# Folding the second layer's DFT over columns a second time, with even and odd outputs side by side in the bank

## The chip, the cores and the metric

The kernel runs on one core of one Trainium2 chip. Its time is device microseconds of one execution; the profile is one further execution, recorded by the hardware profiler.

## The reference, cut to what matters

```python
def _A_ref(x, dft_seq_re, dft_seq_im, dft_hid_re, dft_hid_im):     # FNet mixing: Real(DFT_seq(DFT_hidden(x)))
    a = jnp.einsum("bsd,ed->bse", x, dft_hid_re)
    b = jnp.einsum("bsd,ed->bse", x, dft_hid_im)
    return jnp.einsum("ts,bse->bte", dft_seq_re, a) - jnp.einsum("ts,bse->bte", dft_seq_im, b)

def _B_ref(x, w_gate, w_up, w_down):                                # gated GLU
    g, u = x @ w_gate, x @ w_up
    return (sigmoid(g) * u) @ w_down

x = A_x                                    # 1 x 2048 x 640, float32; the GLU is 1728 wide
for _ in range(2):                         # two layers, the same matrices in both
    x = x + _A_ref(layernorm(x), ...)
    x = x + _B_ref(layernorm(x), ...)
```

## The kernel before, in words

The kernel takes the DFT matrices as inputs but uses their symmetries: cos(n) = cos(N - n), sin(n) = -sin(N - n). Whether the inputs really have them is tested on the chip beside the other work (the *tests*: a part of a matrix is loaded, mirrored parts are subtracted or added on DVE, and ACT sums the squares). A flag at the end decides whether a general, slow path must run; with these inputs it doesn't.

**Rows of x.** The 16 tiles of 128 rows are kept in four blocks of four tiles GA, GB, GC, GD, so that mirrored rows (t, S - t, S/2 - t, S/2 + t) lie on the same partition. Block 1 (`SP`) holds the rows that are their own mirror image, apart from the others in `row`.

**A layer's mixing, folded.** `fold_columns` adds and subtracts the mirrored columns of a row (321 sums `e`, 320 differences `o`, the EC and EH of the code), `fold_rows` normalizes and folds mirrored rows, `fold_join` folds them once more (GB and GD then hold what the even and the odd output rows need) and splits the result into two float16 parts, HI and LO. A float32 product is done as three float16 ones (`PASSES`: HI x HI, HI x LO, LO x HI). Then TensorE works in two steps. `sequence(i, tp)` (line 796) is the DFT over rows for block i, even (EV) or odd (OD) outputs: 18 matmuls of some 256 columns into three banks. Blocks 0 and 1 (ph 0) share banks, as do blocks 2 and 3 (ph 1). `evict_sums` takes the banks out into `z`, again as two parts (line 239 on DVE, line 237 on ACT). `hidden(q, ph)` (line 922 in `product`) is the DFT over columns: z as stationary operand, the 321 columns of the cosine or sine matrix (`h`) as moving operand, 18 matmuls into a pair of banks. `evict_hidden`, `join_hidden` (996) and `add_hidden` (1009) bring the result to x. `hidden_middle` is the same for the rows that are their own image.

Layer 1's mixing is the opening, in float32 for the first step, in an order written out by hand. It splits the cosine and sine matrices and stores the parts in DRAM (`drop_hidden`); layer 2 loads them back (`load_wh_again`).

**Order of the rest.** From then on `steps` is the list of TensorE's work with a planned duration for each step, and every other operation is set into that list, at a planned time (`when`, `run_at`) or at a step (`run`). Each engine runs its own instructions in this order. Layer 1 after its opening: gate and up products (steps "c"), the seven-product form of them ("j", line 1174, whose sums ACT copies out at line 1178 and DVE adds), then down-projections ("d", lines 1316, 1411, 1430; DVE adds to x in line 1304). During the second half of "j" blocks 0 and 1 are folded for layer 2 and stored (`spill`), during the last down-projection blocks 2 and 3. `he` is the index of the first step of layer 2's mixing, `b0` that of its first gate product:

```python
order = [(sequence, 0, EV), (sequence, 1, EV), (sequence, 0, OD), (sequence, 1, OD), (sequence, 2, EV),
         (sequence, 2, OD), (hidden, 0, 0), (sequence, 3, EV), (hidden, 1, 0), (sequence, 3, OD),
         (hidden, 0, 1), (hidden, 2, 0), (hidden, 3, 0), (hidden, 1, 1), (hidden, 2, 1), (hidden, 3, 1),
         (hidden_middle,)]
...
run_at(end + 3, [(fold_join, 3, ALL, (n,)) for n in range(3)])
...
run(he + 2, evictions(0, (EV,)))
```

All DMAs but a few go through one queue (SP). All buffers lie in one large tile in SBUF; `PLACES` lists, in the order of the requests, where each goes. There are eight banks of PSUM, handed out in the order in which they came free. The tests go over stretches of time (`spans`: from, to, weight), spread evenly over the weighted length; each loads in one slot, subtracts two slots later and squares 0.85 of a slot after that.

Of the kernel before, what the change touches and what calls it, by code (L numbers as in the profile page):

```python
# [17 lines left out]
P = 128  # L18
# [13 lines left out]
EC = EH + 1  # L32
EPS = 1e-5
# [8 lines left out]
XF = 2.0**8  # L42
CS = 2.0**14
ZS = 2.0**-1
# [62 lines left out]
273 327 208 343 402 172 367 336 237 332"""  # L107
# [95 lines left out]
def folded(ctx, tc, pool, dram, big, acc, flag, x, ct, wh, wg, wu, wc, wd, out):  # L203
# [5 lines left out]
    hs = pool.tile([P, 1], F32, name="hs")  # L209
    edge = pool.tile([P, 2], F32, name="edge")  # L210
# [100 lines left out]
    def start_identity():  # L311
        nc.vector.tensor_scalar(ident16, ramp, part[:, 34:35], None, op0=OP.is_equal)

        nc.vector.tensor_tensor(hs, ident16[:, 63:64], ident16[:, 64:65], op=OP.add)
        nc.vector.tensor_scalar(hs, hs, -0.5 * CS, CS, op0=OP.mult, op1=OP.add)
        drop("ramp")
        drop("part")
# [258 lines left out]

    def fold_stats(i, g):
        row_stats(quad_tile(i), g, 4 * i + g)
# [8 lines left out]
    def fold_columns(i, k):  # L587

        g = slice(2 * k, 2 * k + 2)
        e, o = (v[:, g] for v in folds(i))  # L590
        xg = X[:, 4 * i : 4 * i + 4, :][:, g]
        a, b = xg[:, :, 1 : EH + 1], xg[:, :, D - 1 : EH - 1 : -1]
        nc.vector.tensor_tensor(e[:, :, :EH], a, b, op=OP.add)
        nc.vector.tensor_tensor(o, a, b, op=OP.subtract)  # L594

    def fold_double(i, k):
# [3 lines left out]
        on.tensor_scalar(e[:, :, EH:], xg[:, :, 0:1], 2.0, None, op0=OP.mult)  # L600
# [43 lines left out]
    def fold_row(n):  # L644
# [5 lines left out]
        if n == 1:  # L650
            nc.vector.scalar_tensor_tensor(f[0:1, :EC], f[0:1, 384 : 384 + EC], t[0:1, GD, 19:20], f[0:1, :EC],
                                           op0=OP.mult, op1=OP.add)
        if n == 2:
            w = take(2, "fw").f16[:, :EC]
            nc.gpsimd.memset(w, 0.0)
            for p in (0, 64):
                nc.scalar.activation(w[p : p + 1], f[0:1, :EC], AF.Copy)
        if n == 3:
            w = held["fw"].f16[:, :EC]
            nc.vector.tensor_tensor(w[32:33], f[0:1, :EC], w[0:1], op=OP.subtract)  # L660
            drop("row")

# [4 lines left out]
    def fold_join(i, v=ALL, do=(0, 1, 2)):  # L667

        for n, (f, ops, fold, key, w) in enumerate(zip(folds(i), ((OP.add, OP.subtract), (OP.subtract, OP.add)),
                                                       (FE, FO), "eo", (EC, EH))):  # L670
            if n not in v:
                continue
            if 0 in do:
                for g, op in zip((GB, GD), ops):
                    nc.vector.tensor_tensor(f[:, g], f[:, GA], f[:, GC], op=op)
            if 1 in do:
                nc.scalar.activation(take_parts(key, i)[:, :, 0, :w], f[:, GB::2], AF.Copy)
                if n:
                    nc.gpsimd.memset(take_parts(key, i)[:, :, :, EH : EH + 1], 0.0)
            if 2 in do:  # L680
                p = take_parts(key, i)
# [1472 lines left out]
```

## Time and profile before

| what | value |
|---|---|
| time, median of 3 runs | 1104.82 us (1104.02 to 1105.79) |
| the profiled execution | 1106.03 us |
| its span in the trace | 1104.2 us |
| instructions | 17528 |
| TensorE busy | 1084.0 us, 6289 matmuls |
| DVE busy | 830.2 us |
| ACT busy | 572.9 us |
| granted TensorE clock | 0.998 |
| layer 2's mixing on TensorE | from 571.66 to 612.46 us of the span |

The span begins with the first recorded instruction. PE is the matmul part of TensorE, PEld its weight loads, which run beside the matmuls. In a line of a timeline stand start, length, engine, line of code, operation, output <- input, shape and count; an idle time before it, and what ended it, stands in brackets. Matmuls are pipelined, so that the length of a group is some 0.16 us longer than the time until the next group starts; in the chain of work the lengths are those up to the next piece. In a list of waits stand the total, the number and the longest.

### The profile page before, as it was taken

The numbers are of one execution on the slowest core, as the hardware profiler recorded it, in microseconds if no ns is written. First come the engines' busy times: TensorE is split into PE (matmuls) and PEld (weight loads), VectorE is DVE, ScalarE is ACT, GpSimd is POOL, SyncE is SP. The second block draws the span as 40 slices with busy tenths as digits, with TensorE's granted clock in tenths as the row PEclk, the third lists the DMA queues.
The fourth block names the chain that finished last, engine by engine and source line by source line (L and its number), as shares of the span: only waits on it lengthen the run. The fifth ranks groups of instructions, "written<-read, shape, count | busy, mean of one in ns | idle before, by whom it ended". The sixth has DMA issues, their size and how long they took to land.

```text
span 1104.2 us, 17528 instructions
## 1 busy us (share of the span) xinstructions
PE 1084.0 (98%) x6289; PEld 626.3 (57%) x6289; DVE 830.2 (75%) x1608; ACT 572.9 (52%) x1109; POOL 154.6 (14%) x250
## 2 busy tenths in 40 slices
PE   6999999999999999999999999999999999999997
PEld 3776444457774444457777844444677444444775
DVE  8996789868448999769887569895895356777962
ACT  7776547765315665555225544476761345555520
POOL 3110153312333151000110100012000010000010
PEclk9999999999999999999999999999999999999999
DMA  8414765366996877756742058645569856666521
GB/s 273 155 61 71 199 184 203 115 193 191 251 249 233 251 250 202 235 174 214 229 141 73 1 62 194 200 154 182 185 163 177 265 180 208 202 196 194 190 88 64
DMA packets 183079, 194.70 MB, mean 176 GB/s; under 512 B 76451, under 2 KB 145474, under 8 KB 182982
## 3 DMA queue, kind: packets, MB, share of 16 engines
q1 hardware_dynamic: 182342, 190.87, 58.8%
q0 software_dynamic: 640, 2.62, 0.6%
q8 instruction: 51, 0.84, 0.3%
q14 instruction: 46, 0.38, 0.1%
HBM read 145.29 MB, written 31.91 MB: 160 GB/s over the span
## 4 chain that ended last, share of the span: by engine, by line
PE 87%; DVE 8%; issue 2%; DMA 1%; ACT 1%; POOL 0%; SPq 0%; DVEq 0%; POOLq 0%; ACTq 0%
PE acc L1174 36%; PE acc L1430 17%; PE acc L1130 14%; PE acc L1316 8%; PE acc L922 4%; PE acc L1411 2%; PE acc L1283 2%; PE acc L834 2%; DVE big L642 1%; DMA big<-big 1%; DVE quad L424 1%; DVE big L239 1%; PE acc L796 1%; DVE big L1509 1%; DVE big L594 0%
## 5 line engine op out<-in xcount | busy, mean ns | idle before, releaser
L1174 PE MATMUL acc<-big 128*128 128x512 f16 x2160 | 467.8, 379 | 2.8 <-ACT big L1178 1.9
L1174 PEld LDWEIGHTS <-big 128*128 128x128 f16 x2160 | 211.3, 98 | 257.8 <-issue 3.5
L1430 PE MATMUL acc<-big 128*128 128x320 f16 x1512 | 213.2, 299 | 0.4 <-DVE big L1304 0.4
L1178 ACT ACTIVATE big<-acc 128x512 f32<-128x512 f32 x160 | 94.0, 593 | 191.9 <-PE acc L1174 167.5
L1430 PEld LDWEIGHTS <-big 128*128 128x128 f16 x1512 | 147.9, 98 | 58.5 <-issue 0.6
L1130 PE MATMUL acc<-big 128*128 128x512 f16 (+1 forms) x900 | 156.6, 336 | 0.0
L1130 PEld LDWEIGHTS <-big 128*128 128x128 f16 x900 | 87.9, 98 | 67.7 <-DVE big L239 0.2
L1481 ACT ACTIVATE big<-big 128x768 f32<-128x768 f32 (+6 forms) x106 | 79.0, 745 | 53.2 <-DVE big L1511 17.0
L1304 DVE SCALAR_TENSOR_TENSOR big<-acc,big 128x320 f32<-128x320 f32 x112 | 53.1, 485 | 53.7 <-PE acc L1411 27.2
L239 DVE SCALAR_TENSOR_TENSOR big<-big 128x640 f16<-128x640 f32 (+7 forms) x94 | 75.9, 830 | 22.5 <-ACT big L237 19.4
L1316 PE MATMUL acc<-big 128*128 128x320 f16 x656 | 89.3, 299 | 0.0
L1391 DVE TENSOR_TENSOR big<-big 128x512 f16<-128x512 f32 x126 | 85.3, 688 | 2.3 <-ACT big L1390 2.3
L1390 ACT ACTIVATE big<-big 128x512 f16<-128x512 f32 x126 | 74.0, 618 | 25.0 <-DVE big L1391 11.1
L237 ACT ACTIVATE big<-big 128x640 f16<-128x640 f32 (+9 forms) x94 | 63.8, 707 | 35.7 <-POOL big L1082 15.8
L1316 PEld LDWEIGHTS <-big 128*128 128x128 f16 x656 | 64.2, 98 | 25.1
L1224 DVE TENSOR_TENSOR big<-big,acc 128x512 f32<-128x512 f32 x40 | 27.3, 682 | 44.4 <-PE acc L1174 30.6
L516 ACT ACTIVATE big<-big 128x384 f16<-128x384 f32 (+2 forms) x56 | 36.0, 667 | 36.6 <-DVE big L501 17.2
L1181 ACT ACTIVATE big<-big 128x512 f32<-128x512 f32 x80 | 49.7, 622 | 9.7 <-DVE big L1224 6.6
L386 POOL DMA_INDIRECT out<-big,rows x8 | 8.6, 1070 | 310.9 <-DVE big L1304 173.5
L1509 DVE TENSOR_TENSOR big<-big 128x512 f32<-128x512 f32 x64 | 46.2, 722 | 5.9 <-DMA big<-in_ct 5.7
L1402 DVE TENSOR_TENSOR big<-big 128x512 f32<-128x512 f32 x72 | 50.1, 697 | 0.1
L439 POOL TENSOR_SCALAR rowt<-rowt 128x1 f32<-128x1 f32 x24 | 13.0, 540 | 242.4 <-ACT big L437 242.4
(199 smaller groups left out, 1230.2 us busy)
## 6 DMA issues: line engine op xcount, KB each, us to landing
big<-in_ct SPq DMA_DIRECT2D x256, 128.0 KB
big<-kept_f SPq DMA_DIRECT2D x63, 320.0 KB
big<-kept_S SPq DMA_DIRECT2D x33, 512.0 KB
big<-kept_w SPq DMA_DIRECT2D x33, 320.0 KB
big<-in_ct SPq DMA_DIRECT2D x32, 256.0 KB
big<-kept_G SPq DMA_DIRECT2D x21, 320.0 KB
kept_S<-big SPq DMA_DIRECT2D x13, 512.0 KB
big<-in_wg SPq DMA_DIRECT2D x19, 320.0 KB
```

The lines of the kernel that those rows point to most:

```text
L237: nc.scalar.activation(dh, src, AF.Copy, scale=s)
L239: nc.vector.scalar_tensor_tensor(dl, src, s, dh, op0=OP.mult, op1=OP.subtract)
L1130: nc.tensor.matmul(ps, w[wp][:, d * P : (d + 1) * P], xt[:, xp, :], start=(d == 0 and wp == HI and xp == HI), stop=(d == ND - 1 and wp == LO))
L1174: nc.tensor.matmul(ps, wt, xt, start=start and n == 0, stop=n == len(todo) - 1, skip_group_check=not start)
L1178: nc.scalar.activation(dst, ps, AF.Copy)
L1304: nc.vector.scalar_tensor_tensor(xe, ps[:, :EH], CB, xe, op0=OP.mult, op1=OP.add)
L1316: nc.tensor.matmul(held["pd", i, e][0][:, :EH], held["t", half, j].parts[hp][:, i * P : (i + 1) * P], held["w", 2, j].parts[wp][:, e * EH ...
L1390: nc.scalar.activation(h, v, AF.Copy)
L1391: nc.vector.tensor_tensor(l, v, h, op=OP.subtract)
L1430: nc.tensor.matmul(ps[:, :EH], a[n][hp][:, i * P : (i + 1) * P], w[n][:, wp], start=fresh and m == 0, stop=m == len(todo) - 1, skip_group_ ...
L1481: nc.scalar.activation(v, v, AF.Square, accum_out=new_sum()[:p])
L1509: nc.vector.tensor_tensor(bd[:, :, 1], bd[:, :, 0], bd[:, :, 1], op=same)
```

## The change

- **The DFT over columns of layer 2 is folded twice.** After the join, `fold_again` folds the 321 sums (and the differences) about their middle: 161 sums and 160 differences, for the even and odd output columns. With `KT2` the row DFT's output has the columns for even outputs in the first 128 partitions of z, those for odd ones in the second 128, and the rest of both in 65 more. `product` then has, for the first two groups, matmuls of 161 columns into one half of the bank each, and for the third one matmuls of 322 into both. Two matrices of 128 rows are half as wide.
- **Evictions** read the bank interleaved (`sums_of_bank`), even column, odd column.
- **The matrices of layer 2** are loaded from the input and split anew (`load_wh2`, `split_wh2`), with factors of one half for the rows that meet themselves (`hs2`, made at the start); the stores and loads of layer 1's parts go.
- **Order in layer 2's mixing**: the even sums of block 3 come two steps earlier, the products and the middle rows are moved, block 3's join runs in halves after the first eviction, and evictions are set anew.
- **Tests**: six more (`load_hidden_fold`, the second fold's symmetry); the tests of the column matrices get a buffer of their own; the spans are new, and the first of them lies at the end of the first "j" of layer 1.
- Scales XF and ZS are halved; the second and later pairs of rows in layer 2's "d" are taken 2 to 5 us earlier; all of PLACES is new.

```diff
-XF = 2.0**8
+XF = 2.0**7
-ZS = 2.0**-1
+ZS = 2.0**-2
...
+        nc.vector.tensor_scalar(hs2[:, 0:1], p, 1.0, 0.5 * CS, op0=OP.is_ge, op1=OP.mult)
+        nc.vector.tensor_scalar(hs2[:, 0:1], hs2[:, 0:1], 0.5 * CS, None, op0=OP.add)
+        for k, op, a, b in ((1, OP.is_le, 31, 32), (2, OP.is_ge, 33, 34), (3, OP.is_le, 30, 31), (4, OP.is_ge, 33, 33)):
+            for c, v in ((hs2[:, k : k + 1], a), (part[:, 36 + k : 37 + k], b)):
+                nc.vector.tensor_scalar(c, p, float(v), 0.5 * CS, op0=op, op1=OP.mult)
+        nc.vector.tensor_tensor(hs2[:, 1:5], hs2[:, 1:5], part[:, 37:41], op=OP.add)
...
+    def fold_again(to, f, r):
+        c, every = EH - 2 * r, (slice(None),) * (len(f.shape) - 1)
+        for n, to_c, op in ((HE + 1, 0, OP.add), (HE, HE + 1, OP.subtract)):
+            nc.vector.tensor_tensor(to[(*every, slice(to_c, to_c + n))], f[(*every, slice(0, n))],
+                                    f[(*every, slice(c, c - n, -1))], op=op)
...
-    KT = (((0, P), (P, P), (2 * P, EC - 2 * P)),) * 2
+    KT = (0, P), (P, P), (2 * P, EC - 2 * P)
+    KT2 = (0, P), (EC - P, P), (P, EC - 2 * P)
...
+    def load_wh2(r, d):
+        s = take(3, "hr", r, d).f32
+        for p, row, n in (((0, r, P),), ((0, 32 + r, P),), ((0, P + r, 33), (33, r, 32)))[d]:
+            nc.sync.dma_start(s[p : p + n, :EC], wh[r, row : row + n, :EC])
...
     def product(ps, ph, r, at, m):
+        for d, (_, n) in enumerate(KT):
+            o = ps[:m, : EC + 1 if steps else EC]
+            if steps and d < 2:
+                c = (r + d) % 2
+                o = ps[:m, c * (HE + 1) : (c + 1) * (HE + 1)]
+            ws = [w[:n, : o.shape[1]] for w in held["h", r, d].parts]
...
+    def sums_of_bank(ps):
+        return ps[:, : EC + 1].rearrange("p (h k) -> p k h", h=2) if steps else ps[:, :EC]
...
             order = [(sequence, 0, EV), (sequence, 1, EV), (sequence, 0, OD), (sequence, 1, OD), (sequence, 2, EV),
-                     (sequence, 2, OD), (hidden, 0, 0), (sequence, 3, EV), (hidden, 1, 0), (sequence, 3, OD),
-                     (hidden, 0, 1), (hidden, 2, 0), (hidden, 3, 0), (hidden, 1, 1), (hidden, 2, 1), (hidden, 3, 1),
-                     (hidden_middle,)]
+                     (sequence, 3, EV), (sequence, 2, OD), (hidden, 0, 0), (hidden, 0, 1), (sequence, 3, OD),
+                     (hidden, 1, 0), (hidden, 1, 1), (hidden, 2, 0), (hidden, 3, 0), (hidden_middle,),
+                     (hidden, 2, 1), (hidden, 3, 1)]
...
-        when(t + 60 + 2 * q, load_wh_again, *divmod(q, 3))
+        when(t + 4 + 2 * q, load_wh2, *divmod(q, 3))
+        when(t + 12 + 2 * q, split_wh2, *divmod(q, 3))
...
+    join = [[(fold_join, 3, ALL, (n,), (k,)) for n in range(1, 4)] for k in range(2)]
+    run(he + 2, [(evict_sums, 0, EV, 0), (fold_join, 3, ALL, (0,)), *join[0], *evictions(0, (EV,))[1:], *join[1]])
     run(he + 4, evictions(0, (OD,)))
+    run(he + 6, evictions(1, (EV,)))
+    run(he + 8, [(evict_hidden, 0, 0)])
+    run(he + 9, [(evict_hidden, 0, 1), (join_hidden, 0, 0), (add_hidden, 0, 0), (norm_stats_dve, 0),
+                 (norm_stats_act, 1), (join_hidden, 0, 1)])
+    run(he + 10, [(rstd_power, norm_t(0, 2), 2, nc.vector), *evictions(1, (OD,)),
+                  (rstd_step, norm_t(0, 2), 2, XS, nc.vector), (add_hidden, 0, 1), (norm_stats_dve, 2)])
...
+    run(he + 14, [(evict_hidden, 3, 0), (norm_apply, 0, True), (norm_apply, 1), (norm_parts, 0), (norm_parts, 1),
+                  (norm_stats_act, 3), (norm_scale, 2, 2)])
...
-            u = d0 + ((2, 20, 47, 57) if first else (6, 20, 46, 56))[i]
+            u = d0 + ((2, 20, 47, 57) if first else (6, 18, 42, 51))[i]
...
+    spans = [(d[0] - 40, d[0] - 14, 0.9), (d[0] + 6, d[0] + 38, 0.5), (d[0] + 100, d[1] - 43, 0.37), (d[1] - 43, d[1] - 3, 0.75),
+             (d[1] - 3, d[1] + 47, 0.3), (c - 11, c + 39, 0.9), (c + 39, d2 - 28, 0.8), (d2 - 28, d2 - 4, 0.85), (d2 + 6, d2 + 28, 0.4),
+             (j2 + 4, j2 + 57, 0.9), (j2 + 57, e2, 0.95), (e2, e2 + 25, 0.7)]
```

More of the change, by code (lines that the diff above doesn't have):

```diff
@@ L665, in drop_rev, with fold_join @@
             drop("rev", k)
-    def fold_join(i, v=ALL, do=(0, 1, 2)):
-        for n, (f, ops, fold, key, w) in enumerate(zip(folds(i), ((OP.add, OP.subtract), (OP.subtract, OP.add)),
-                                                       (FE, FO), "eo", (EC, EH))):
+    def fold_join(i, v=ALL, do=(0, 1, 2, 3), only=ALL):
+        for n, (f, ops, fold, key) in enumerate(zip(folds(i), ((OP.add, OP.subtract), (OP.subtract, OP.add)),
+                                                    (FE, FO), "eo")):
             if n not in v:
@@ L903, in load_wh, with split_wh2 @@
             nc.sync.dma_start(s[n : n + 1, :EC], wh[r, 0:1, :EC])
-    def load_wh_again(r, d):
-        v = take(3, "h", r, d).f16.rearrange("p (q c) -> p q c", q=2)
-        nc.sync.dma_start(v[: KT[r][d][1], :, :EC], kept["h", r, d])
+    def load_wh2(r, d):
+        s = take(3, "hr", r, d).f32
+        for p, row, n in (((0, r, P),), ((0, 32 + r, P),), ((0, P + r, 33), (33, r, 32)))[d]:
+            nc.sync.dma_start(s[p : p + n, :EC], wh[r, row : row + n, :EC])
+    def split_wh2(r, d, do=ALL):
+        s = held["hr", r, d].f32
+        if d < 2:
+            c = (r + d) % 2
+            v = held["h", r, d] if ("h", r, d) in held else take(2, "h", r, d)
+            h, l = (w[:, : HE + 1 - c] for w in v.parts)
+            split(h, l, s[:, c:EC:2], hs2[:, 0:1] if (r, d) == (0, 0) else CS, do)
+            for q in do if c else ():
+                nc.gpsimd.memset(v.parts[q][:, HE : HE + 1], 0.0)
+        else:
+            n = KT[d][1]
+            h, l = (w[:n] for w in (held["h", r, d] if ("h", r, d) in held else take(3, "h", r, d)).parts)
+            for c in range(2):
+                k, to = (1, 2, 4, 3)[2 * r + c], slice(c * (HE + 1), c * HE + HE + 1)
+                split(h[:, to], l[:, to], s[:n, c:EC:2], hs2[:n, k : k + 1], do)
+            for q in do:
+                nc.gpsimd.memset((h, l)[q][:, EC : EC + 1], 0.0)
+        if 1 in do:
+            drop("hr", r, d)
     def split_wh(r, d, do=ALL):
-        n = KT[r][d][1]
+        n = KT[d][1]
         v = (held["h", r, d] if ("h", r, d) in held else take(3, "h", r, d)).f16
@@ L947, in drop_hidden @@
             for d in range(3):
-                if ("h", r, d) not in kept:
-                    keep(held["h", r, d].f16.rearrange("p (q c) -> p q c", q=2)[: KT[r][d][1], :, :EC], "h", r, d)
                 drop("z", r, d)
@@ L1777, in folded @@
                          (fold_scale, 3, k, k + 1, nc.vector), (fold_double, 3, k), (fold_rows, 3, k)], 0.0 if k else 2.0)
-    run_at(end + 3, [(fold_join, 3, ALL, (n,)) for n in range(3)])
     t = start_of(0, "d", 1)
@@ L1988, in folded @@
         when(at_test(k) - 0.2, take, CK, "room", k)
+    slow = [n for n, test in enumerate(tests) if test in more]
+    when(at_test(slow[0]) - 0.2, take, 5, "room", 3)
     for n, (load, test, key) in enumerate(tests):
-        when(at_test(n), within, n % 3, load, *key)
-        when(at_test(n + 2), within, n % 3, test, *key)
-        when(at_test(n + 2.85), square_rest)
+        k, late = (3, 1.0) if n in slow else ((n - sum(m < n for m in slow)) % 3, 0)
+        when(at_test(n), within, k, load, *key)
+        when(at_test(n + 2 + late), within, k, test, *key)
+        when(at_test(n + 2.85 + late), square_rest)
+    when(at_test(slow[-1] + 3.9), drop, "room", 3)
     for k in range(3):
```

143 lines of the change are left out of this document (81 added, 62 removed), and 64 rows, old and new, of the table PLACES.

## The prediction

> **What bounds the kernel now.** I read the page first (busy shares), then TensorE's own waits, then the order of time through layer 2's DFT on each engine.
>
> ```profile
> span 1104.2 us, 17528 instructions
> PE 1084.0 (98%) x6289; PEld 626.3 (57%) x6289; DVE 830.2 (75%) x1608; ACT 572.9 (52%) x1109; POOL 154.6 (14%) x250
> L1174 PE MATMUL acc<-big 128*128 128x512 f16 x2160 | 467.8, 379 | 2.8 <-ACT big L1178 1.9
> ...
> PE acc L1174 <- ACT big L1178: 1.9, 1, 1.9
> PE acc L1174 <- DMA big<-big: 0.9, 1, 0.9
> ...
> PE acc L796 <- DVE big L239: 0.6, 1, 0.6
> PE acc L922 <- ACT big L971: 0.5, 1, 0.5
> PE acc L1430 <- DVE big L1304: 0.4, 1, 0.4
> ```
>
> TensorE is busy 1084.0 of 1104.2 us. After the opening it waits only in these five places, 4.3 us in all. So TensorE work that is taken out is time, as long as DVE and ACT, which hand banks back, keep up. The stretch that the change works on, on TensorE (start, length, last bracket: idle time before):
>
> ```profile
> 571.66 2.47 PE L796 MATMUL acc<-big 128*128 128x257 f16 x21
> ...
> 581.90 2.78 PE L796 MATMUL acc<-big 128*65 128x256 f16 x24 [0.56 <-DVE big L239]
> 584.52 2.63 PE L922 MATMUL acc<-big 128*128 128x321 f16 x18
> ...
> 593.39 14.97 PE L922 MATMUL acc<-big 128*128 128x321 f16 x108
> 608.19 1.28 PE L540 MATMUL acc<-ident,big 128*128 128x128 f16 x20
> 610.00 2.63 PE L922 MATMUL acc<-big 128*97 128x321 f16 x18 [0.53 <-ACT big L971]
> 612.46 6.71 PE L1130 MATMUL acc<-big 128*128 128x256 f16 x60
> ```
>
> Layer 2's DFT runs from 571.66 to 612.46, 40.8 us: eight row sums (L796), nine column products (L922), one pair of transposes (L540). The gate matmuls follow at 612.46.
>
> **The shorter matmuls.** Rows of the chain (start, length) and of weight loads (busy us, mean ns):
>
> ```profile
> 584.68 2.46 PE acc L922 x18
> 587.15 1.97 PE acc L796 x18
> ...
> 619.18 1.12 PE acc L540 x20
> 850.82 9.21 DMA big<-big
> ...
> L540 PEld LDWEIGHTS <-big 128*128 128x128 f16 x80 | 4.9, 98 | 0.3
> L922 PEld LDWEIGHTS <-big 128*97 128x97 f16 x24 | 3.0, 124 | 0.9 <-issue 0.6
> ```
>
> A product takes 18 matmuls of 321 columns in 2.46 us, 137 ns each. The transposes take 20 of 128 columns in 1.12 us, 56 ns each, and each has its own weight load. Straight between the two, 0.42 ns a column, 161 columns take 70 ns. A product of layer 2 becomes 6 of 322 columns and 12 of 161: 6 x 0.137 + 12 x 0.070 = 1.66 us, 0.80 less. Eight of them: 6.4 us. The ninth (the middle rows) loads 97 weight columns at 124 ns. Its short matmuls cost between 70 ns (saved: 0.80) and 124 (0.15); I take 0.5. TensorE work saved: 6.9 us.
>
> That a weight load lasts 98 ns, longer than 70, doesn't bound them by the transposes' row: loads overlap there, 80 busy for 4.9 us, 61 ns each. The Trainium skill ("TensorE: Matmul & The Clock Gate", Back-to-back issue gap) speaks against it: a real stream of load and matmul pairs is said to sustain about 81 ns at 128 columns. By that page the short ones would not go below 81 ns and the eight products would save about 1.1 us less; the trace's 56 ns for the same size disagrees, so the row decides.
>
> **Does the rest keep up?** DVE and ACT in that stretch, and a test's two DVE lines from elsewhere:
>
> ```profile
> 576.90 1.02 DVE L642 SCALAR_TENSOR_TENSOR big<-big,quad 128x321 f32<-128x321 f32 x2 [0.79 <-ACT big L636]
> 577.84 1.69 DVE L675 TENSOR_TENSOR big<-big 128x321 f32<-128x321 f32 x4
> 579.60 1.65 DVE L682 TENSOR_TENSOR big<-big 128x642 f16<-128x642 f32 x2
> 581.16 3.67 DVE L239 SCALAR_TENSOR_TENSOR big<-acc,big 128x512 f16<-128x512 f32 x6
> ...
> 597.45 0.83 DVE L996 TENSOR_TENSOR big<-big 128x642 f32<-128x642 f32 x1
> 598.31 1.56 DVE L1009 TENSOR_TENSOR big<-big 128x642 f32<-128x642 f32 x2
> ...
> 606.45 1.71 DVE L465 TENSOR_TENSOR big<-big 128x640 f16<-128x640 f32 x2
> ...
> 576.78 0.55 ACT L638 ACTIVATE big<-big,quad 128x320 f32<-128x320 f32 x1
> 580.29 2.99 ACT L237 ACTIVATE big<-acc 128x512 f16<-128x512 f32 x6
> 599.97 0.74 ACT L437 ACTIVATE big<-big 128x640 f32<-128x640 f32 x1 [3.47 <-DVE big L1009]
> ...
> 601.56 0.19 ACT L438 ACTIVATION_READ_ACCUMULATOR big<-big,rowt 128x1 f32 x1
> 601.65 1.40 ACT L971 ACTIVATE big<-acc 128x321 f32<-128x321 f32 x4
> ...
> 396.44 0.68 DVE L1509 TENSOR_TENSOR big<-big 128x512 f32<-128x512 f32 x1
> 397.15 0.50 DVE L1511 TENSOR_TENSOR big<-big 128x128 f32<-128x128 f32 x2
> ```
>
> Each of these is divided by its count: 0.41 us for a fold of 321, 0.61 for a DVE eviction of 512 and 0.50 on ACT, 0.35 for an ACT eviction of 321, 1.8 for row statistics on ACT. A fold of 161 lies between 128 columns (0.25) and 321 (0.41); I take 0.25, as it is nearest the 128.
>
> I lay the new order out by hand from the same starting point, a row sum at 1.97 us (L796 in the chain; the second, with three matmuls more, 2.3).
> - Block 3's rows are ready on DVE at 577.9, as before. The first eviction of even sums now goes ahead of the join: done 578.5, before the fifth row sum needs that bank (about 581). The 0.56 us wait goes.
> - Join, 4 x 0.41: 580.2. Second fold of the even half, 4 x 0.25: 581.2. ACT copy and DVE rest: first operand at 581.6, second 582.0. The sixth row sum (block 3, even; it was the eighth step, now it starts at 581.8) meets them, no wait worth counting.
> - Two more evictions (583.3), the odd half's fold and split (585.1), then the odd sums' first bank at 585.8. The third part of the seventh row sum wants that bank at 585.1: wait 0.7. This is what is late next.
> - First product 586.4, second 588.1; the second needs its third operand, evicted at 588.8 behind two others: wait 0.35. Ends 590.1. Last row sum to 592.1.
> - On DVE and ACT from 590.1: eviction, join, add (593.7), statistics (ACT 595.6), power on POOL with the three odd evictions on DVE in that time (598.0), scale, add, statistics (601.4), split to 603.3. On TensorE four products; the third waits 0.6 for a bank of the odd sums (596.8). Middle to 601.3, a product to 602.9, transposes at 602.9 with the second row just ready.
> - The last product wants a bank that ACT frees at 604.9, behind row 3's statistics: 0.8, where before it was 0.53.
>
> New waits 2.4, old 1.1: the stretch gives 6.9 - 1.3 = 5.6 us. Rounding between rows eats 0.1: 5.5.
>
> **The other parts.** Rows of the opening, of the tail of layer 1, and two windows (busy us of PE, PEld, DVE, ACT, POOL, then clock, DMA share, GB/s):
>
> ```profile
> 7.48 0.83 DVE L593 TENSOR_TENSOR big<-big 128x640 f32<-128x640 f32 x1 [1.48 <-ACT big L363]
> ...
> 428.97 1.08 ACT L1178 ACTIVATE big<-acc 128x512 f32<-128x512 f32 x2 [2.22 <-DVE big L682]
> ...
> 203.00:229.00 26.00, 26.00 (x121) 11.72 (x120) 18.11 (x30) 19.37 (x41) 8.32 (x20) 1.00 0.49 143
> ...
> 652.00:692.00 40.00, 40.00 (x187) 18.10 (x186) 36.96 (x72) 17.70 (x33) 0.00 (x0) 1.00 0.81 157
> ```
>
> The reads of a bank as even and odd interleaved (runs of two) appear in no row. Reversed rows cost nothing: a 642 fold is 0.83 us forward (L996), and the fold that reads a row reversed, 640, also 0.83 (L593). Lower bound no cost, upper bound twice: 0.35 more on each of the 11 evictions that ACT does from 590.1 to 606.6, where the layout above fills 12.9 of its 16.5 us, so 3.5 us idle take up most of it. I take none, as the reversed rows are the nearest.
>
> The eleven one-column operations that make scale vectors at the start are bounded by zero and 1.48 us, the idle time of DVE that follows them while ACT is awaited; I cost them nothing. Without that cover they would put off the first fold one for one.
>
> Layer 2's column matrices are loaded from the input in the last down-projection of layer 1 and split there (8 pieces of 161 on ACT and DVE, 2 to 3 us of each, 8 small POOL fills); six stores at the start and six loads go. SP issues eight loads for six. These are wanted 70 us later: nothing. Second folds of blocks 0 and 1 add 2 x 1.64 us to DVE near 385-430, and the row of block 1 two operations.
>
> Tests go from 100 to 106, and where they lie comes from the written spans (length times weight, shared evenly). By it, 319-449 us holds 10 instead of 16, the rest of layer 1's tail 539-572 none instead of 4; 203-229 six instead of none, 642-692 twelve instead of five. A test costs DVE 1.13 us (L1509 to the end of L1511), ACT a square, SP two to four loads. So 319-449 loses 6.8 us of DVE and gains 4. The 1.9 us wait near 429 is ACT's copy held by block 0's old last split (L682), with DVE full: between all of it staying and all going, I take 1.0 gained. Late next there: the same copy for the next column group. The 0.4 us in the tail: 0.2 gained. The 0.9 us wait for a transpose (DMA ending 860.07 above) goes, since that pair's work is issued 5 us earlier: 0.9.
>
> Against it: at 203-229 ACT has 6.6 us free and gets four squares by 229; its copies of sums sit behind them, and TensorE needs each within 3.2 us (fifteen matmuls of 0.216): 0 to 0.9 for each square, I take 0.5 in all. At 652-692 DVE is idle 3.0 us and gets some 8 tests, 9 us, for 6 that it had, 7: a lag, 0.4. New places in memory change which buffer waits for which: 0.3 (bounds -0.5 to +2).
>
> Sum: -5.5 - 1.0 - 0.2 - 0.9 + 0.5 + 0.4 + 0.3 = -6.4. The profiled execution took 1106.03 us (span 1104.2), 1.2 above the median of 1104.82. 1106.03 - 6.4 = 1099.6 there, 1098.4 at the median.
>
> **Rivals.**
> - *Covers hold better than laid out*: with no wait left after the opening it would be 1104.8 - 6.9 - 4.3 = 1093.6; with all of the old ones gone and the 2.4 us of new ones in the stretch left, 1096.0. For it: DVE's total work before the stretch falls. Against: the bank waits follow from the order alone.
> - *Interleaved reads cost double*: 3.9 us on ACT, half of it uncovered, and 1 on DVE: 1101.3. Against: reversed rows are free.
> - *Weight loads bound the short matmuls* at 98 ns: 8 x 12 x 0.028 = 2.7 less, 1101.1. Against: the transposes.
> - *Tests stall the copies*: at 203-229 a whole square each (3.7), and at 692 a lag beyond 6.3 us (the 3.7 us between test and square, 2.6 of a copy's slack): 1103-1104, no change measurable.
> - *Slower*: ACT's evictions become the bound of the stretch. If an interleaved bank read took four times 0.35, eleven of them add 11.5 us, 8.0 above ACT's idle time: 1106.4. It turns slower from 1.25 us each. Only an unseen price speaks for it; no row does.
>
> **How the numbers follow.** Main case 0.53 (its own range 1096.6-1100.6), better 0.14, doubled reads 0.11, weight loads 0.04, tests 0.11, slower 0.07. Some 0.2% (2.2 us) is what a measurement of this kernel tells from no change, so faster is below 1102.6: 0.53 + 0.14 + 0.11 + 0.03 = 0.81; same 0.12; slower 0.07. The range 1095.3-1103.6 leaves out the slower case and the far part of the tests.
>
> **What would show it.** Right: L922's successor with 12 matmuls of 161 near 70 ns, products of 1.66 us; the gate matmuls about 35.3 us after the first row sum, for 40.8; no wait before the fifth row sum, 0.7 before the end of the seventh; ACT's evictions of 322 near 0.37 us; TensorE waits elsewhere under 3 us; DVE idle reappearing in 319-449. Wrong: short matmuls near 98 ns, evictions near 0.7 us, or copies of sums released late at 215-230 or 690-715.

## The result, and the profile after

The changed kernel takes 1110.55 us (median of five runs, 1109.84 to 1112.21) for 1104.82 before: 1.0053 of it, 95% interval 1.0039 to 1.0068. That is slower by 5.7 us, where the prediction had 1098.4. The profiled execution has a span of 1110.4 us (before: 1104.2). From the page of the changed kernel, and behind it TensorE's waits (us in total, times, longest):

```profile
span 1110.4 us, 17626 instructions
PE 1079.0 (97%) x6289; PEld 622.5 (56%) x6289; DVE 840.6 (76%) x1663; ACT 573.5 (52%) x1131; POOL 151.4 (14%) x254
```

```profile
PE acc L1237 <- ACT big L1241: 5.3, 3, 2.7
...
PE acc L1237 <- DMA big<-big: 2.6, 1, 2.6
...
PE acc L1379 <- DVE big L241: 1.8, 4, 0.6
PE acc L1237 <- DMA big<-kept_G: 1.2, 1, 1.2
PE acc L825 <- DVE big L241: 0.8, 1, 0.8
PE acc L976 <- DVE big L241: 0.8, 1, 0.8
...
PE acc L976 <- ACT big L1032: 0.5, 1, 0.5
```

TensorE's work did fall, from 1084.0 to 1079.0 us. What grew is its waiting, and most of it is not in the DFT: the seven products (L1237; L1174 before) wait for copies (L1241), for a DMA transpose (big<-big) and for a form's load (kept_G; a form is here one set of operands of the seven products, kept in DRAM), and the down-projection of layer 1 (L1379) for its operands. The DFT stretch of layer 2 itself, on TensorE, and its copies on ACT:

```profile
577.38 2.46 PE L825 MATMUL acc<-big 128*128 128x257 f16 x21
...
591.82 0.82 PE L825 MATMUL acc<-big 128*65 128x256 f16 x6 [0.83 <-DVE big L241]
592.48 3.50 PE L976 MATMUL acc<-big 128*128 128x161 f16 x36
...
602.91 6.00 PE L976 MATMUL acc<-big 128*128 128x161 f16 x63 [0.81 <-DVE big L241]
608.74 1.28 PE L549 MATMUL acc<-ident,big 128*128 128x128 f16 x20
610.52 1.82 PE L976 MATMUL acc<-big 128*128 128x161 f16 x18 [0.49 <-ACT big L1032]
612.18 3.99 PE L1193 MATMUL acc<-big 128*128 128x256 f16 x35
```

```profile
L1032 ACT ACTIVATE big<-acc 128x322 f32<-128x322 f32 x11 | 4.0, 447 | 0.2 <-PE acc L976 0.2
```

From 577.38 to 612.18 it takes 34.8 us, for 40.8 before: 6.0 less. It begins 5.7 us later than before, and so the gate matmuls begin at the same time, 612.18 for 612.46. What was gained here had been lost ahead of it, and more was lost after it.

To place the losses I take, for each pair of successive matmuls, the distance of their starts less the distance that this shape keeps undisturbed (216 ns for 512 columns, 137 for 321, 70 for 161), and add these up by stretch. Undisturbed stretches come out at 0 to -0.9, from rounding. All runs of this study, in us; the median is over all executions, the other columns are from the one that was profiled:

| kernel | median | 203-262 | 332-430 | 430-580 | DFT, 580-613 | 613-790 | 790-end |
|---|---|---|---|---|---|---|---|
| before | 1104.8 | 0.0 | 1.8 | 0.1 | 1.4 | -0.4 | 0.2 |
| changed | 1110.6 | 4.3 | 2.6 | 0.3 | 2.6 | 6.8 | -0.4 |
| e2, none at 203-229 | 1121.9 | -0.2 | 3.7 | 5.9 | 2.6 | 16.1 | -0.3 |
| e3, old gate stage | 1115.3 | 3.8 | 2.6 | -0.5 | 2.6 | 9.6 | 0.4 |
| e23, both | 1120.7 | -0.2 | 3.6 | 2.7 | 2.6 | 14.1 | 0.1 |
| e1, all old spans | 1106.9 | -0.2 | 7.7 | 2.4 | 2.6 | -0.4 | -0.9 |
| e5, loads only | 1109.5 | 3.8 | 3.9 | -0.3 | 2.6 | 4.4 | -0.4 |
| e6, work only | 1099.9 | -0.2 | 2.2 | -0.3 | 2.6 | -0.4 | -0.3 |
| e7, untested, changed | 1096.2 | -0.2 | -0.2 | -0.5 | 2.7 | -0.5 | -0.9 |
| e8, untested, before | 1104.4 | 0.0 | -0.2 | 0.7 | 0.7 | -0.4 | -0.9 |
| e9, small loads | 1099.4 | -0.2 | 2.3 | -0.5 | 2.6 | -0.4 | -0.1 |
| e12, five less | 1106.4 | 4.2 | 2.6 | -0.5 | 2.6 | 1.6 | -0.4 |
| e10, first new spread | 1108.7 | -0.2 | 1.6 | 6.8 | 2.6 | 6.3 | 0.0 |
| e11, second | 1112.4 | -0.2 | 1.3 | -0.5 | 7.1 | 3.6 | 5.3 |
| e13, third, late | 1108.0 | -0.2 | 2.8 | 4.0 | 2.6 | 2.5 | 2.5 |
| e14, third, early | 1125.7 | -0.2 | 2.8 | 3.3 | 2.6 | 21.4 | -0.4 |
| e15, fourth | 1116.0 | -0.2 | 1.2 | -0.1 | 2.7 | 7.4 | 6.2 |

The changed kernel loses 4.3 us at 203-262 and 6.8 at 613-790, where before nothing was lost. The second stretch is that of layer 2's gate and up products, called the gate stage below; by the distances 7.1 are lost at 692-720, and rounding makes the sum 6.8. Both lie where the tests were spread anew. In the first place, on SP's queue and on ACT:

```profile
216.76 2.52 SPq L1565 DMA_DIRECT2D big<-in_ct  x4
219.33 0.46 SPq L751 DMA_DIRECT2D big<-in_ct  x1
...
220.44 6.28 SPq L1565 DMA_DIRECT2D big<-in_ct  x8
```

```profile
224.91 0.68 ACT L239 ACTIVATE big<-big 128x516 f16<-128x516 f32 x1 [2.22 <-DMA big<-in_ct]
...
227.04 0.57 ACT L1241 ACTIVATE big<-acc 128x512 f32<-128x512 f32 x1
```

L1565 is a test's load of four times 128 KB, L751 the layer's own load of a DFT matrix. Issued at 219.33, behind a test's, it is what ACT waits for until 224.91, 2.22 us with nothing else to do; the copy of sums (L1241) stands behind that split in ACT's order and runs at 227.04, and TensorE waits for copies there. This wait is 1.5 of the 4.3 us. Most of the rest, 2.8, lies at 236-262, where the down-projection waits for its operands (the four waits of L1379 above). The loads of its weights stand behind tests' loads on SP as well and are issued 7.6 us later, before (first fence) and after (second):

```profile
225.08 2.53 SPq L1022 DMA_DIRECT2D big<-in_wd  x5
```

```profile
232.64 0.88 SPq L1085 DMA_DIRECT2D big<-in_wd  x2
```

In the second place, on the gate stage's queue, before (first fence) and after (second), then what DVE, ACT and TensorE wait for:

```profile
658.13 6.89 SPq L533 DMA_TRANSPOSE big<-big  x1
...
678.91 4.78 SPq L533 DMA_TRANSPOSE big<-big  x1
...
686.10 2.03 SPq L1103 DMA_DIRECT2D big<-kept_G  x1
```

```profile
649.64 2.62 SPq L1565 DMA_DIRECT2D big<-in_ct  x4
...
653.60 10.01 SPq L1565 DMA_DIRECT2D big<-in_ct  x8
663.81 4.63 SPq L542 DMA_TRANSPOSE big<-big  x1
...
686.66 6.49 SPq L542 DMA_TRANSPOSE big<-big  x1
...
695.59 1.81 SPq L1166 DMA_DIRECT2D big<-kept_G  x1
```

```profile
695.39 10.26 PE L1237 MATMUL acc<-big 128*128 128x512 f16 x39 [2.59 <-DMA big<-big]
706.84 4.71 PE L1237 MATMUL acc<-big 128*128 128x512 f16 x21 [1.19 <-DMA big<-kept_G]
712.74 3.61 PE L1237 MATMUL acc<-big 128*128 128x512 f16 x16 [1.20 <-ACT big L1241]
...
709.30 0.42 DVE L1588 TENSOR_REDUCE cmax<-big 128x1 f32<-128x256 f32 x1 [2.60 <-DMA big<-in_ct]
...
711.27 0.84 ACT L1544 ACTIVATE big<-big 128x768 f32<-128x768 f32 x1 [3.97 <-DVE big L1591]
...
712.12 1.07 ACT L1241 ACTIVATE big<-acc 128x512 f32<-128x512 f32 x2
```

The stage starts at the same time in both kernels, so the rows compare directly: the transposes are issued 5.7 and 7.8 us later, the load of a form (kept_G) 9.5. TensorE then waits for just these. The third wait is one step further: DVE waits for a test's load, ACT's square for DVE, and the copy that TensorE wants stands behind the square.

### The profile page after: what moved, and what is told of

It is laid out like the page before. It is cut to its first block, busy times and chain, and to the rows that moved or that the text cites. A ratio compares the mean times of both kernels' runs of the same rounds, so it can differ in the third digit from the quotient of the medians.

```text
span 1110.4 us, 17626 instructions
## 1 busy us (share of the span) xinstructions
PE 1079.0 (97%) x6289; PEld 622.5 (56%) x6289; DVE 840.6 (76%) x1663; ACT 573.5 (52%) x1131; POOL 151.4 (14%) x254
## 2 busy tenths in 40 slices
DMA packets 182400, 194.71 MB, mean 175 GB/s; under 512 B 76413, under 2 KB 144794, under 8 KB 182302
## 4 chain that ended last, share of the span: by engine, by line
PE 69%; DVE 13%; DMA 8%; ACT 4%; SPq 3%; issue 2%; POOL 1%; DVEq 0%; ACTq 0%; POOLq 0%
PE acc L1237 31%; PE acc L1493 14%; PE acc L1193 10%; PE acc L1379 7%; DMA big<-in_ct 3%; PE acc L976 2%; PE acc L1474 2%; PE acc L1346 2%; SPq L1565 2%; DVE big L241 1%; DMA kept_c<-big 1%; DMA big<-in_wd 1%; DVE wmax L232 1%; DVE big L656 1%; DVE big L1454 1%
## 5 line engine op out<-in xcount | busy, mean ns | idle before, releaser
L1237 PE MATMUL acc<-big 128*128 128x512 f16 x2160 | 470.1, 380 | 9.1 <-ACT big L1241 5.3
L1237 PEld LDWEIGHTS <-big 128*128 128x128 f16 x2160 | 211.6, 98 | 266.0 <-issue 11.7
L1241 ACT ACTIVATE big<-acc 128x512 f32<-128x512 f32 x160 | 93.0, 590 | 170.4 <-PE acc L1237 170.0
L1544 ACT ACTIVATE big<-big 128x768 f32<-128x768 f32 (+7 forms) x112 | 80.9, 723 | 53.9 <-DVE big L1574 14.9
L241 DVE SCALAR_TENSOR_TENSOR big<-big 128x640 f16<-128x640 f32 (+9 forms) x97 | 76.0, 805 | 25.1 <-ACT big L239 21.7
L1379 PE MATMUL acc<-big 128*128 128x320 f16 x656 | 90.1, 299 | 2.0 <-DVE big L241 1.8
L239 ACT ACTIVATE big<-big 128x640 f16<-128x640 f32 (+11 forms) x97 | 64.7, 695 | 35.4 <-POOL big L1145 14.1
L1379 PEld LDWEIGHTS <-big 128*128 128x128 f16 x656 | 64.2, 98 | 27.9 <-issue 3.0
L526 DVE TENSOR_TENSOR big<-big 128x384 f16<-128x384 f32 (+2 forms) x56 | 40.9, 743 | 3.9 <-ACT big L525 3.9
```

What stands on the lines that cost most here:

```text
L239: nc.scalar.activation(dh, src, AF.Copy, scale=s)
L241: nc.vector.scalar_tensor_tensor(dl, src, s, dh, op0=OP.mult, op1=OP.subtract)
L1237: nc.tensor.matmul(ps, wt, xt, start=start and n == 0, stop=n == len(todo) - 1, skip_group_check=not start)
L1241: nc.scalar.activation(dst, ps, AF.Copy)
L1379: nc.tensor.matmul(held["pd", i, e][0][:, :EH], held["t", half, j].parts[hp][:, i * P : (i + 1) * P], held["w", 2, j].parts[wp][:, e * EH ...
L1544: nc.scalar.activation(v, v, AF.Square, accum_out=new_sum()[:p])
```

## The experiments

"Theory A" below is what the last paragraphs say: the tests in their two new places hold up the layer's own loads and copies. The first four runs only move tests; buffers keep their places.

**e2, e3, e23, e1.** In e2 the first span is left out (`spans2 = spans[1:]`). In e3 the three spans of the gate stage are replaced:

```diff
-spans[5:8]   # c-11..c+39 .9, c+39..d2-28 .8, d2-28..d2-4 .85
+[(c + 5, j, 0.7 * even), (j, d2 - 7, even)]   # the same total weight
```

e23 does both, e1 takes all spans of the kernel before for the 106 tests.

> The changed kernel, but no symmetry test lies in block one's turned stretch (203-229 us): all 106 are spread over the remaining spans, and buffer places stay as they are. Theory A (test loads and test work there hold up the layer's own loads and copies): the 4.3 us that TensorE waits between 203 and 262 us go, the rest stays, about 1106.3 us. Rival B (the new places in memory make buffers wait for each other): places are the same, so the time stays within 1 us of 1110.5. Rival C (the loss is in the gate stage alone and the wait at 203-262 is made up elsewhere): 1109-1110.5.

> The changed kernel, but the tests of layer 2's gate stage lie as before the change: none until 5 us into the stage, weight 0.7 to 1, in the same total weight, so that all tests outside 640-775 us keep their times. Theory A: the 7.1 us that TensorE loses at 692-720 go, also the 1.7 us in which matmuls ran at half speed; the tail of that span, now denser, costs up to 1: about 1103.5-1104.5 us. Rival B (new places): within 1 us of 1110.5. Rival D (the slow matmuls at 696 us come by themselves, not from the wait ahead of them): 1.7 us stay, 1105-1106.

> The changed kernel with both repairs: no tests at 203-229 us, and the gate stage's as before the change. Theory A: the losses add, 4.3 + 7.1 us come back, 1099-1100 us, faster than before the change by about 5. Rival B (new places): 1109-1111. Rival E (the second fold brings nothing in the end, the tests only hid that): 1104-1106, as before the change.

> The changed kernel with all 106 tests in the spans that the kernel before used (203-229 us none, layer 1's tail as before, the gate stage as before). Theory A: 1099-1101 us; against the kernel with both repairs alone it has the wait of some 2 us near 429 us back or not, which shows what the thinning of 319-449 us was worth (0 to 1.5). Rival B (new places): 1109-1111.

Measured: 1121.94 (ratio to before 1.0148, interval 1.0129 to 1.0167), 1115.27 (1.0095, 1.0079 to 1.0110), 1120.68 (1.0148, 1.0134 to 1.0162) and 1106.87 (1.0018, 1.0009 to 1.0027). No theory's times came. But the table shows that half of it holds: without tests at 203-229 the 4.3 us there are gone, to -0.2. The tests, spread over the rest, cost more there: 5.9 at 430-580 and 16.1 in the gate stage (e2). With the old spans the gate stage is free (-0.4), but 332-430 loses 7.7, where DVE now has the second folds of blocks 0 and 1 as well; that these are the cause is not tested alone. Rival B is out too: with the same places in memory, losses of 0 to 16 us appear in one stage, by the tests' spread alone.

**e5, e6, e7, e8.** For the tests that were put at 203-229 and 640-692 (18 of 106) either the work or the load is left out; in the other two kernels all spread tests go.

```diff
+def early(n):
+    return at_test(n) < d[0] or c - 11 <= at_test(n) < c + 39
 for n, (load, test, key) in enumerate(tests):
     when(at_test(n), within, k, load, *key)             # e6: not for early ones
     when(at_test(n + 2 + late), within, k, test, *key)  # e5: not for early ones
     when(at_test(n + 2.85 + late), square_rest)         # e5: not for early ones
```

> The changed kernel; of the six tests at 203-229 us and the twelve or so at 640-692 only the loads are issued, their DVE and ACT work is left out, and the verdict of the tests is fixed. The earlier set showed that the 4.3 us at 203-262 go with those tests, but that moving the tests of either place elsewhere costs as much or more there. Theory A (the loads, in SP's queue and on the DMA engines ahead of the layer's own transfers, cost the time): 1108-1110.5. Rival C (the tests' DVE and ACT work costs it): near 1100.

> The opposite: the same tests do their DVE and ACT work on what lies in their buffers (cleared by POOL when they are taken), but their loads are not issued; the verdict of the tests is fixed. Theory A: the 4.3 and 7.1 us go, 1099-1101. Rival C: 1108-1110.5. If both halves lie near 1104 to 1106, DVE's and ACT's work and the loads share the loss.

> The changed kernel with all 106 spread tests left out, loads and work (the rows 0 and 1024 are still tested, the verdict is fixed). What is left is the fold with its own waits. Theory F (the fold gains what its stretch showed, the tests spend it): 2.5 us of waits in the DFT stretch stay and at most 2 elsewhere, 1095-1097, and 6 to 8 below the kernel before without its tests. Rival G (the fold itself is behind some of the loss, through second folds on DVE in 319-449 and through its places): 1098 or more, within 4 of the kernel before without tests.

> The kernel before with all 100 spread tests left out in the same way. Its waits near 429 (1.9) and in layer 1's tail (0.4) should go, the 0.9 at 860 and 1.1 in the DFT stretch may stay: 1101-1103. With the run of the changed kernel without tests it gives the worth of the fold alone (theory F: 6 to 8 us, rival G: under 4).

Measured: loads alone 1109.50 (1.0040, 1.0027 to 1.0054; five runs of 1107.5 to 1110.6, and a sixth took 3014 us, for which I have no explanation), work alone 1099.87 (0.9961, 0.9948 to 0.9974), no tests 1096.24 (0.9922, 0.9910 to 0.9935), the kernel before without tests 1104.43 (0.9999, 0.9990 to 1.0008). So it is the loads that cost the time: with the DVE and ACT work of all 106 tests in place but 18 loads gone, the changed kernel is 4.7 us faster than before. That loads alone come so close to the changed kernel's time is in part chance: they lose 4.4 us in the gate stage instead of 6.8, but 1.3 more at 332-430, where TensorE ran at half speed after a wait (last section). Whether the 2.4 us between 4.4 and 6.8 are the tests' work behind its late loads, or scatter between executions, is open. And the fold is worth what its stretch shows. TensorE's waits without tests, of the changed kernel:

```profile
PE acc L825 <- DVE big L241: 0.8, 1, 0.8
PE acc L976 <- DVE big L241: 0.8, 1, 0.8
PE acc L976 <- ACT big L1032: 0.5, 1, 0.5
```

After the opening these three are all. From the first row sum to the last matmul it takes 518.5 us (569.42 to 1087.94), the kernel before without tests 524.5 (569.41 to 1093.94): 6.0. The medians differ by 8.2; 1.8 of the rest lies behind the last matmul (8.7 us to the end of the span there, 6.8 here), and why is not settled. The kernel before, expected at 1101 to 1103 without its tests, hardly moves in time. In the trace its last matmul does start 3.3 us earlier (1093.94 for 1097.25), but 1.7 of that is lost again behind it.

**e9, e12, e10.** What about a load costs: its slot in SP's queue, or its bytes? In e9 the early tests' loads keep slot and order and move a sixteenth of the columns:

```diff
-nc.sync.dma_start(v[:, g], bass.AP(ct.tensor, ..., [[256, 8], [d * S, 16], [1, 256]]))
+nc.sync.dma_start(v[:, g, :16], bass.AP(ct.tensor, ..., [[256, 8], [d * S, 16], [1, 16]]))
```

e12 leaves tests 36, 40, 44, 48 and 52 out; e10 is a new spread.

> The changed kernel; the same tests (six or seven at 203-229 us, eleven at 640-692) keep their DVE and ACT work, on buffers that POOL cleared, and each of their loads is issued as before, in the same place of SP's queue, but moves a sixteenth of the columns, so some 30 KB instead of 512 KB for a test; the verdict is fixed. Work alone ran at 1099.9. Theory A1 (the place in SP's queue and the issue time of 0.6 us each delay the layer's own loads): 1106-1110. Theory A2 (the bytes on the DMA engines delay them): 1100-1102.

> The changed kernel with five of the some thirty tests of the gate stage (535-665 on the plan's clock) left out altogether, spread over the stage; all others stay where they are; the verdict is fixed. So far 24 and 25 tests in this stage (before, and the changed kernel with the old spans) cost it nothing, some 30 cost 7 to 10 us, 31 cost 16. Theory N (the number of tests in the stage decides, as the DMA engines are full there): of the 7.1 us at most 2 stay, 1103.5-1105.5. Theory P (the early place of the first twelve decides, ahead of the transposes): 5 or more stay, 1108-1110.5.

> The changed kernel with all 106 tests spread anew: none at 203-229; five in the first gate matmuls of layer 2 (about 615-640 us), where the DMA engines are 3% busy; some 25 in the gate stage, from its sixth microsecond on; none around 395-445; the first down stage of layer 2 as before the change. If the number of test loads in a stage that is full of transfers is what costs, 1097-1100, faster than both kernels: 2.6 us of waits in the DFT stretch stay, 0 to 2 near 425, 0 to 1 in the gate stage. If tests cost wherever they are put, 1104 or more. If DVE can't take five more at 615-640 (16 of 25 us are in use), a wait of 1 to 3 us shows there.

Measured: small loads 1099.42 (0.9954, 0.9941 to 0.9967), as fast as without them. So it is the bytes: the number of packets is the same (182401 for 182400), and the bytes fall from 194.71 to 186.42 MB. The windows (us; PE, PEld, DVE, ACT and POOL busy; clock, DMA share, GB/s) of the changed kernel, then of e9:

```profile
640.00:690.00 50.00, 50.00 (x233) 22.67 (x232) 40.11 (x79) 24.62 (x47) 0.00 (x0) 1.00 0.79 150
690.00:720.00 30.00, 25.02 (x107) 10.56 (x106) 22.39 (x44) 10.46 (x23) 0.00 (x0) 0.94 0.81 219
```

```profile
640.00:690.00 50.00, 50.00 (x233) 22.63 (x232) 45.78 (x90) 24.61 (x49) 0.00 (x0) 1.00 0.61 123
690.00:720.00 30.00, 30.00 (x140) 13.58 (x139) 26.25 (x54) 18.91 (x42) 0.71 (x3) 1.00 0.51 161
```

DVE does more there in e9 (45.78 us of 50 for 40.11) and TensorE loses nothing; the DMA share falls from 0.79 to 0.61 and from 0.81 to 0.51. All but 4 of the 194.71 MB go through one hardware queue (packets, MB, share of 16 engines):

```profile
q1 hardware_dynamic: 181662, 190.87, 58.1%
```

The Trainium skill ("DMA: Bandwidth & Descriptors", Queues, rings and completion order) says that each DMA engine consumes the descriptors of a queue in order. By that, an engine begins its part of a form's load only after its part of a test's 512 KB issued ahead of it. The runs agree, with the tests' work in place: 1099.9 without the loads (e6), 1099.4 with a sixteenth of their bytes (e9), 1110.6 with all of them.

Five tests less in the gate stage: 1106.42 (1.0017, 1.0005 to 1.0029), between the two theories' times. The 7.1 us become 1.9, as theory N had it, but the run does not tell number from place: of the three loads of L1565 that SP issued ahead of the transpose at 663.81, one is among the five. The first new spread: 1108.69 (1.0033, 1.0020 to 1.0046). Its gate stage is free after 660, but two waits took the place of the old ones:

```profile
PE acc L1193 <- DMA big<-big: 4.8, 1, 4.8
PE acc L1493 <- DMA big<-kept_f: 4.2, 1, 4.2
```

By the order of the rows, the first are the gate stage's transposes, behind the work of tests on DVE at 637-647, and the second loads of the down-projection's stages, behind tests' loads at 472-488; no run tests either alone.

**e11, e13, e14, e15.** A second spread, then a pair that has the same 27 tests in the gate stage, early or late, and a fourth spread put together from places that had cost little:

```diff
-(c - 11, c + 39, 0.092), (c + 39, d2 - 4, 0.27)    # e13: 5 tests planned at 640-690, 22 after
+(c - 11, c + 39, 0.3), (c + 39, d2 - 4, 0.146)     # e14: 15 tests planned at 640-690, 12 after
```

> The changed kernel with all 106 tests in a second new spread. The first one lost 4.9 us at 652 (DVE work of tests at 637-647 ahead of the operands of the layer's first transposes, which TensorE then awaits) and 4.4 at 500 (loads of tests at 472-488 ahead of stage loads), and nothing in the gate stage with its 25 tests. Now three loads at the end of the DFT stretch, with only one test's work before 650; seven for eleven tests at 455-495; 24 to 25 in the gate stage; five more in layer 2's later stages, which have cost nothing so far. If bytes in crowded stages and DVE work on that chain are the whole of it: 2.6 us in the DFT stretch, 1 to 2 near 370-420, 0 to 1 at 500, 0 to 1 after 800, so 1098-1101, faster than both kernels. If there is no room for 106 tests without loss, 1104 or more.

> The changed kernel with all tests in a third spread: none at 203-229, 27 in the gate stage, of which only some 5 lie before its fortieth microsecond (640-690 us), the other 22 after it; in the tail of layer 1 those near 465-480 go to 440-460; the last ones end later, in the last down-projection. Theory P (loads cost where the transposes and the layer's own loads fill the DMA engines): 0 to 1 us lost in the gate stage, 1098-1101.5, faster than both kernels. Theory N (the number in the stage): 27 lies between 25 and 30, so 2 to 6 lost there, 1101-1106.

> The same spread and the same 27 tests in the gate stage, but 15 of them lie before its fortieth microsecond (640-690 us) and 12 after it. Theory P: 6 us or more lost at 690-720, so at least 5 above the run with the late ones. Theory N: the same time as the run with the late ones, within 1.5 us.

> The changed kernel with the tests where earlier runs lost little: layer 1's tail as in the second new spread (1.3 us lost there), the gate stage as in the first (25 tests from its sixth microsecond on, denser after the fortieth; nothing lost), layer 2's down stage and later products at the changed kernel's density, the last ones up to 38 us into the last down-projection. Each density is some 4% higher, as 106 tests have to fit. If places decide and these are free: 1.3 near 400-420, 2.6 in the DFT stretch, up to 2 elsewhere over the 1096.2 without tests, so 1098-1101. If 106 tests don't fit beside the fold's own work, 1103 or more.

Measured: second spread 1112.43 (1.0068, 1.0054 to 1.0082), which lost 7.1 in the DFT stretch and 5.3 after 790. In the DFT, three tests' work stands on DVE at 599.8-604.6 and on ACT at 604.2-605.6, not one as planned, ahead of what the transposes and the last product want. Late 1108.02 (1.0032, 1.0021 to 1.0043), early 1125.73 (1.0196, 1.0183 to 1.0210): 17.7 us between the same tests in the same stage. SP lags behind the plan: by 690 it has issued nine tests' loads in the early one, where 15 were planned, and five in the late one. TensorE's waits in the early one, a window of it, and the same window of the late one:

```profile
PE acc L1237 <- ACT big L1241: 13.8, 6, 9.3
PE acc L1237 <- DMA big<-kept_G: 7.6, 1, 7.6
```

```profile
690.00:720.00 30.00, 11.83 (x41) 4.50 (x42) 18.63 (x40) 8.80 (x19) 0.00 (x0) 0.72 0.80 211
```

```profile
690.00:720.00 30.00, 30.00 (x141) 13.61 (x140) 23.79 (x46) 17.25 (x38) 0.47 (x2) 1.00 0.61 196
```

So with the number the same, the place makes 17.7 us: SP issues the first form's load at 691.85 in the early run and at 673.01 in the late one. Theory N can't be the whole account, but neither can theory P: the late run lost 2.5 us in the stage, as N had it, and not the 0 to 1 of P, and missed its time by 6.5. Place is not all that counts. The fourth spread, built from it, took 1115.98 (1.0108, 1.0087 to 1.0129; its profiled execution, 1112.2, was its fastest), with 7.4 us lost in a gate stage of 26 tests and 6.2 after 790; e10, with 25 tests there in almost the same places, lost none after 660. What sets these two apart is open: the kinds of tests that fall there differ, and so does their phase against the layer's loads. No spread of the 106 tests was found that beats the kernel before; with the old spans it is 0.2% slower.

## Why the prediction was wrong, step by step

- *Shorter matmuls*: right. The last product's 18 matmuls begin at 610.52 and the gate's at 612.18: 1.66 us, as worked out. The middle rows' short ones keep 70 ns as well, though they load 97 weight columns, so they saved the full 0.8, the upper end, and weight loads bound nothing.
- *Does the rest keep up*: right. Waits of 0.83, 0.81 and 0.49 where 0.7, 0.6 and 0.8 were laid out; the 0.35 of the second product did not come, and the old 0.56 is gone. 34.8 us for 35.3.
- *Interleaved reads of a bank*: free. Eleven of 322 columns take 4.0 us, 0.36 each. The rivals that hung on them fall.
- *The 0.9 us wait at 860*: gone, as said. But it is gone in the kernel before without tests too (e8), so that the earlier issue removed it is not shown. *The scale vectors* at the start: the seven products begin 0.36 us later (154.78 for 154.42), which can't be told from scatter: in the other runs of the changed kernel, with the same opening, they begin between 153.8 and 155.7.
- *Fewer tests at 319-449 free DVE*: wrong in sign. The wait near 429 grew to 2.7, where 1.0 was to be gained. Without tests it is gone altogether (e7), and with the old tests beside the second folds the stretch loses 7.7, 1.4 of it at half speed (e1); so the thinning seems to have kept it from getting worse. (A test's work on DVE is 1.21 us by the rows shown, not 1.13, which moves no term.)
- *Against it* is the step that failed, 0.5 for 203-229 and 0.4 for 652-692; measured 4.3 and 7.1. It counted squares on ACT and work on DVE, which cost nothing as long as their data are there in time (e6), and gave the loads no price, although the quoted windows showed the DMA engines at 0.49 and 0.81 and the text named two to four loads a test on SP. What it left out is that the layer's own loads and transposes queue behind them (e9), and that a late load holds whatever is ordered behind its consumer. With these two terms at their measured size the sum would be -6.4 - 0.9 + 11.4, or +4.1. The other terms, measured against predicted, add 2.2: the wait near 429 1.8, layer 1's tail, a new wait at 814 and the opening 0.4 each, less 0.5 for the DFT stretch and 0.3 for the places. That is +6.3, for +6.2 between the two spans.
- *New places*: cost nothing. Without tests no wait is left outside the opening and the DFT stretch.
- Of the rivals, "tests stall the copies" named the right two places but through squares and DVE, and put them at no measurable change. The one on the slower side was another. The sign that the prediction had set for itself, copies released late at 215-230 and at 690-715, did come.

## What to carry to other kernels

Background work that is moved has to be priced on every resource that it uses, its transfers first: in the two places here the DMA engines had been busy 0.49 and 0.81 of the time, and half a megabyte at a time ahead of loads that were wanted soon cost 4 and 7 us, though DVE and ACT could do the work itself at no cost (e6). Look at what stands behind the moved transfer in the queue, and at who waits for that. And before such work is spread, run the kernel once without it: that shows in one run what the change is worth (6 us up to the last matmul here) and how much the spread costs.

## What the hardware showed beside that

After the 2.59 us wait at 695.39 TensorE ran at half speed for 3.4 us, some 1.7 us of the loss at 692-720. Windows of the changed kernel, the clock third from the end:

```profile
692.80:695.39 2.59, 0.00 (x0) 0.03 (x1) 2.38 (x4) 0.58 (x2) 0.00 (x0) 1.00 1.12 240
696.30:699.70 3.40, 3.40 (x10) 1.16 (x9) 3.10 (x8) 1.45 (x4) 0.00 (x0) 0.50 0.48 121
700.30:703.70 3.40, 3.40 (x17) 1.57 (x16) 2.71 (x5) 1.49 (x3) 0.00 (x0) 1.00 0.94 278
```

The same kernel's 2.7 us wait near 428 had no such effect. The Trainium skill ("TensorE: Matmul & The Clock Gate", Why this matters for your kernels) asks for no idle gap over some 3 us; here one of 2.59 was followed by half speed, and one slightly longer was not.

The 17 traces together show what the difference is. In each of them the recorded changes of the clock lie whole multiples of 3.41 us apart, so the time can be cut into slots of that length. Between 160 and 1080 us there are 41 slots at full clock in which TensorE was idle for more than 1.3 us. None of the 25 with at most 1.93 us was followed by half speed; 15 of the 16 with 1.96 us or more were, and the exception is the slot near 428, with 2.03. No stretch at half speed in that time began without one of these 15 ahead of it, so that rival D of e3 is out. By these rows the length of a wait does not decide, but how much of it falls into one slot. The wait of 1.96 us in e11 lies within one (first fence), that of 3.14 us in e15 is divided between two, with 1.93 in the second (second fence):

```profile
603.79:607.20 3.41, 1.46 (x20) 1.21 (x17) 1.61 (x5) 3.41 (x10) 2.63 (x9) 1.00 0.15 50
607.21:610.62 3.41, 3.41 (x19) 2.31 (x17) 1.38 (x3) 2.83 (x6) 0.01 (x1) 0.50 0.50 147
```

```profile
711.30:714.71 3.41, 1.48 (x7) 0.68 (x7) 1.48 (x4) 2.95 (x7) 0.00 (x0) 1.00 0.98 295
714.71:718.12 3.41, 3.41 (x17) 1.57 (x16) 2.51 (x7) 3.35 (x10) 0.48 (x2) 1.00 0.17 61
```

So a wait of 2 us can cost 1.7 more, and where it falls in the slot is chance: the wait near 428, 2.69 us in the changed kernel and 2.73 in e5, was followed by half speed only in e5.
